# Gated mix of a spectral filter and an MLP on one core: dense products of the first chunk ahead of the first DFT tiles, and VectorE's exchange of halves partly on ScalarE

## The chip, the core and the metric

The kernel runs on one core of a Trainium2 chip. The metric is the device time of one execution in microseconds (us); lower is better. The core has five engines that each work through their own instructions in order: TensorE (PE, with PEld its weight loads), VectorE (DVE), ScalarE (ACT), GpSimd (POOL) and SyncE (SP). Here SP issues nearly all DMA transfers, which 16 DMA engines carry out; POOL does nothing.

## What is computed

```python
def reference(A_x, A_w_r, A_w_i, B_x, B_w1, B_b1, B_w2, B_b2, gate_w):
    x = A_x                                     # [1, 2048, 512]
    g = sigmoid((x * gate_w).sum(-1, keepdims=True))
    X = rfft2(x, axes=(-2, -1)) * (A_w_r + 1j * A_w_i)
    a = irfft2(X, s=(2048, 512), axes=(-2, -1))
    h = gelu(einsum("bsd,df->bsf", x, B_w1) + B_b1)      # F = 1792
    b = einsum("bsf,fd->bsd", h, B_w2) + B_b2
    return g * a + (1 - g) * b
```

Both branches read the same 2048 tokens of 512 features: the spectral branch filters over tokens and features by DFTs, the dense branch is a two-layer MLP, and a gate per token mixes them.

## The kernel before

**Precision.** Every operand of a matrix product is split into a high and a low part (`split`, L407 to 412: ScalarE copies to the high part, VectorE subtracts to get the low part), and a product is three matmuls: high by high, high by low, low by high (`prods`, L371). All matmuls are recorded at one line, L369, so the profile tells them apart by the names of their tiles.

**Spectral branch.** The 2048 tokens are 16 tiles of 128 (`forward(j)`, L495), done in the order `NORD` = 0, 4, 8, 12, 1, 5, 9, 13, 2, ... For each tile VectorE forms sums and differences of mirrored features (`eo`, L502), ScalarE and VectorE split them (`eoh` L507, `eol` L509), TensorE does the DFT over features (`pd`, 12 matmuls of 258 columns, with the table `cf`), ScalarE and VectorE split the result (`xh` L539, `xl` L540), and TensorE does a DFT of 128 over tokens (`py`, 6 matmuls with a table `tf` loaded for each tile). ScalarE copies one half of it (`pys`, L559); VectorE adds (L560) and subtracts (L563) into the tile `Y[j]`. The subtraction exchanges the lower and upper 64 partitions, so it is two instructions of 64 partitions. The first two rows of every tile pair go by a small DMA to `own` (L565); `own_rows` (L571) corrects them by a small product (`pown`) and 16 small DMAs put them back (L589). Radix-4 butterflies over the 16 tiles, the filter (`filt`, L671), and butterflies back (`stage4`, L706) are all VectorE's; then come the inverse products `pz` and `pa` (`inverse`, L710), where `v` and `z` are the split operands.

**Dense branch.** The MLP (`mlp`, L782) works in 4 chunks of 512 tokens and two halves of the hidden features (7 blocks of 128 each). For each half and chunk: 7 `ph` (12 matmuls of 512 columns; gelu at L803, then a split into `g`), then 4 `po` of 7 x 3 matmuls. The split tokens of a chunk (`mxh`, `mxl`) are made from four tiles (`split_1`, L475; for chunk 0 from the tiles 0, 4, 8, 12 that the spectral branch loads too), stored to memory (`keep_x`, L481) and read again for the second half of the hidden features (L493). Weights are loaded and split on the way (`load_w`, L777; `wa`, `wb`; two landing buffers of each kind). Partial sums go through memory (`bacc`).

**What sets the order.** No loop order is executed as written. Every operation is a `Step` with an engine, an assumed cost, a lag, buffers and a rank (`Graph.add`, L150), and a planner (`schedule`, L188) simulates the engines: an engine that is free takes the ready step of lowest rank whose buffers find a slot. The result is one fixed order of instructions for each engine. `slots` (L320) says how many buffers of each kind there are, `most` (L324) how many of them a class may hold. Ranks are `FEED` = 1, `BULK` = 5, `EARLY` = 0.5, `FIRST` = 0.3 for the first three tiles. Semaphores that make an instruction wait are put in behind the planner. The DMA transfers go round a set of eight semaphores, so a ninth transfer is issued only when an earlier one has landed.

At the start eight matmuls of zeros (`warm`, L424) run on TensorE while the tables `cf` (L434), four weights and the first tile (by ScalarE's queue, L432) are loaded; then the first tile's `pd` follows.

Of the kernel before, what the change touches and what calls it, by code (L numbers as in the profile page):

```python
# [17 lines left out]
P = 128  # L18
# [112 lines left out]

class Step:
# [11 lines left out]
class Graph:  # L144
# [5 lines left out]
    def add(self, eng, cost, lag, emit, reads=(), writes=(), rank=1):  # L150
# [4 lines left out]
        def parts(x):  # L155
            b, p = x if isinstance(x, tuple) else (x, None)
            return b, range(len(b.wrote)) if p is None else (p,)
# [149 lines left out]
def tile_kernel(ctx: ExitStack, tc: tile.TileContext, xt, w1, w2, b1, b2, x0g, wf, wrev, out, consts):  # L307
# [12 lines left out]
    slots = {"xr": 3, "wra": 2, "wrb": 2, "t2k": 6, "e2": 4, "z": 4, "ttab": 3, "xhl": 2, "wa": 2 * FA, "wb": 2 * FA, "hid": 2 * FA,  # L320
# [3 lines left out]
    most = {("pm", "ph"): 2, ("pm", "po"): 2, ("pm", "py"): 3}  # L324
# [12 lines left out]

    FIRST, FEW = 0.3, 3
# [20 lines left out]
    def dma(emit, kb, reads, writes, rank=FEED):  # L359
        return add("sp", kb / 390, 2.2, emit, reads, writes, rank)  # L360

    def dma_act(emit, kb, reads, writes):
        return add("act", 0.4, kb / 390 + 2.2, emit, reads, writes, 0)
# [40 lines left out]
    def t2k(name, n=ND, cls=None):  # L404
        return buf("t2k", [P, 2, n], F32, name, cls=cls)
# [26 lines left out]
    dma_act(lambda: act.dma_start(x0.ap().rearrange("p a b -> p (a b)")[:, :NQ * P + NQ], x0g), 258, [], [x0])  # L432
    for c in range(2):
        dma(lambda c=c: raw(cf(c, 0), cf_d[c]), 272, [], [(cft, k) for k in (c, 8 + c, 10 + c)], 0)  # L434
    XF[NORD[1]] = load_x(NORD[1], "f")

    def tiny(emit, reads, writes):
        return add("vec", 0.1, 0.1, emit, reads, writes, -1)
# [42 lines left out]
    def keep_x(c):  # L481
        for k, b in zip("hl", X[0, c]):
            dma(lambda k=k, b=b: sp.dma_start(xs[c, k].ap(), b.ap().bitcast(F32)), 1024, [b], [xs[c, k]], 6)
# [11 lines left out]
    def forward(j):  # L495
        first = j == 0
        feed = FIRST if j in NORD[:FEW] else FEED
# [3 lines left out]
        for s, op in ((0, ALU.add), (1, ALU.subtract)):  # L501
            v(lambda s=s, op=op: vec.tensor_tensor(eo.ap()[:, s], x.ap()[:, 0:2], x.ap()[:, 2:4], op=op), 256, [x],  # L502
              [(eo, s)], -1 if first else feed)
        for k in (0, 1) if first else (slice(0, 2),):
# [3 lines left out]
              -1 if first else feed)  # L508
            v(lambda k=k: vec.tensor_tensor(l.ap()[:, k], eo.ap()[:, k], h.ap()[:, k], op=ALU.subtract),  # L509
              256 * len(ps), sub[0] + sub[1], sub[2], feed)  # L510
# [35 lines left out]
        pys = t2k(f"pys{j}", cls="pys")  # L546
# [12 lines left out]
        a(lambda: act.activation(pys.ap()[:, 0], py[0].ap()[:, :ND], AF.Copy), 257, [py[0]], [pys], 0)  # L559
        v(lambda: vec.tensor_tensor(Y[j].ap()[:, 0], py[1].ap()[:, :ND], pys.ap()[:, 0], op=ALU.add), 257, [py[1], pys], [(Y[j], 0)], 0)  # L560
        lo, up = slice(0, HP), slice(HP, P)
        for k, (o, i) in enumerate(((lo, up), (up, lo))):
            v(lambda o=o, i=i: vec.tensor_tensor(Y[j].ap()[o, 1], py[1].ap()[i, :ND], pys.ap()[i, 0], op=ALU.subtract),  # L563
              257, [pys, py[1]], [(Y[j], 1 + k)], 0)
# [3 lines left out]
    own = buf("bb", [2 * NJ, 2, NE], F32, "own", parts=NJ + 1)  # L568
    add("vec", 0.1, 0.1, lambda: vec.memset(own.ap()[:, :, ND:], 0.0), [], [(own, NJ)], 3)

    def own_rows():  # L571
        t = buf("ttab", [2 * NJ, 2, 2, 2, 2 * NJ], F32R, "fx")
        dma(lambda: raw(t.ap(), fx_d), 32, [], [t], 3)
        oh, ol = (buf("z", [2 * NJ, 2, 512], F32R, f"own{k}") for k in "hl")
        a(lambda: act.activation(oh.ap()[:, :, :NE], own.ap(), AF.Copy), 514, [own], [oh], 2)
        v(lambda: vec.tensor_tensor(ol.ap()[:, :, :NE], own.ap(), oh.ap()[:, :, :NE], op=ALU.subtract), 514, [own, oh], [ol], 2)
# [8 lines left out]
        m(fix, NE, 12, [t, oh, ol], [ps], FEED)  # L585
        r = t2k("ownr")
        a(lambda: act.activation(r.ap()[:2 * NJ], ps.ap()[:, :, :ND], AF.Copy), 514, [ps], [r], 2)
# [189 lines left out]
    def load_w(n, f):  # L777
        t = buf("wr" + n, [P, D], F32, f"w{n}r{f}")
        dma(lambda: sp.dma_start(t.ap(), (w1 if n == "a" else w2)[f]), 256, [], [t], EARLY if f < FA else 2)
        W[n, f] = split(f"w{n}{f}", "w" + n, [P, D], t, lambda x: x, 512, EARLY if f < FA else 3)  # L780

    def mlp(half, c):  # L782
# [23 lines left out]
        for q in range(NQ):  # L806
# [3 lines left out]
            for n in (slice(0, 2 * P), slice(2 * P, 4 * P)) if end else (slice(0, 4 * P),):  # L810
                ps = buf("pm", [P, n.stop - n.start], F32, f"po{half}_{c}{q}{n.start}", pool=pp, cls="po")
# [35 lines left out]

    ORDER = (2, 3, 0, 1)
    LATE = (0, 1)

    for n, j in enumerate(NORD):
# [3 lines left out]
        if j == 12:  # L855
            keep_x(0)
# [6 lines left out]
    for p0 in range(0, P, 32):  # L863
# [3 lines left out]
            700, [gsc], [gt])  # L867
# [75 lines left out]
```

## Time and profile before

| | |
|---|---|
| median of 3 runs | 402.66 us (401.99 to 402.69) |
| the profiled execution | 402.02 us, of which its span 400.2 us |
| TensorE busy | 388.6 us, 97% of the span |
| VectorE busy | 328.4 us, 82% |
| ScalarE busy | 162.4 us, 41% |
| DMA | 65.63 MB, mean 164 GB/s |
| granted TensorE clock | 0.994 |

The page's numbers come from one execution. Its span runs from the first to the last instruction; the time of the execution is 1.8 us longer. Busy shares are averages over stages. The chain of work that ended last is followed back from the last instruction; a row of it gives start, duration and the work. Rows in order of time give start, duration, engine, line, operation, output and inputs, and in brackets the idle time before them with what ended it. SPq and ACTq are the queues on which DMA transfers are issued. In the first slices the clock column reads 1.00 although matmuls take twice their later time, so the durations are the better guide there.

### The profile page before, as it was taken

The page shows a single profiled execution, that of the slowest core. Times are in us where ns is not written, and L with a number is a line of the kernel's source. Part 1 is how long each engine was busy: PE and PEld are TensorE (multiplying, and loading weights), DVE is VectorE, ACT ScalarE, POOL GpSimd, SP SyncE. Part 2 cuts the span into 40 slices and gives each one's busy share as a digit, 9 for nine tenths or more (in the row PEclk, how much of TensorE's full clock was granted, in tenths as well). Part 3 has the DMA queues.
Part 4 walks back from the last instruction along what each step waited for, and adds up shares of the span by engine and source line. Part 5 has one row for each costly group of instructions (what it writes and reads, how often), then busy time and mean ns, then how long its engine had stood idle before and what let it go on. Part 6 is the DMA issues. An engine that isn't in the chain of part 4 may idle for free.

```text
span 400.2 us, 5515 instructions
## 1 busy us (share of the span) xinstructions
PE 388.6 (97%) x1961; PEld 329.5 (82%) x1961; DVE 328.4 (82%) x687; ACT 162.4 (41%) x267; POOL 0.2 (0%) x4
## 2 busy tenths in 40 slices
PE   7789999999999999999999999999999999999996
PEld 5668889887888888888888898888899888888885
DVE  4998999999999999999999779987999996322223
ACT  5567555636651354156236520334422354004300
POOL 0000000000000000000000000000000000000000
PEclk9998999999999999999999999999999999999999
DMA  8896455696049133743952285451756444510011
GB/s 294 330 316 199 138 156 159 176 382 212 5 109 359 64 104 131 266 141 95 312 178 102 79 311 164 134 162 47 261 153 176 154 126 150 231 52 26 2 52 52
DMA packets 31675, 65.63 MB, mean 164 GB/s; under 512 B 3744, under 2 KB 10240, under 8 KB 29600
## 3 DMA queue, kind: packets, MB, share of 16 engines
q1 hardware_dynamic: 31504, 65.03, 48.9%
q8 instruction: 15, 0.25, 0.2%
q10 hardware_dynamic: 144, 0.26, 0.2%
q14 instruction: 12, 0.10, 0.1%
HBM read 46.26 MB, written 18.88 MB: 163 GB/s over the span
## 4 chain that ended last, share of the span: by engine, by line
PE 79%; DVE 12%; DMA 5%; issue 2%; ACT 1%; SPq 0%; DVEq 0%; ACTq 0%
PE ph L369 34%; PE po L369 33%; PE pz L369 6%; PE pa L369 3%; PE pd L369 2%; DVE y L563 2%; DVE eo L502 2%; DVE eol L509 1%; DMA war<-in_w 1%; DVE y L560 1%; DMA cf<-cf 1%; DMA xs0h<-mxh 1%; DMA bb<-bacc 1%; DMA ba<-bacc 1%; PE py L369 1%
## 5 line engine op out<-in xcount | busy, mean ns | idle before, releaser
L803 ACT ACTIVATE ph<-ph,b1t 128x512 f32<-128x512 f32 x56 | 37.0, 661 | 85.1 <-PE ph L369 83.7
L823 ACT ACTIVATE o<-po,b2t 128x512 f32<-128x512 f32 x16 | 11.0, 690 | 46.2 <-PE po L369 43.2
L836 DVE SCALAR_TENSOR_TENSOR o<-gb,po 128x512 f32<-128x512 f32 (+1 forms) x9 | 5.7, 629 | 24.5 <-PE po L369 24.5
L688 DVE TENSOR_TENSOR m<-y,wf 128x514 f32<-128x514 f32 x32 | 21.4, 690 | 0.0
L369 PE MATMUL pd<-cf,eoh 128*128 128x258 f32 x128 | 19.3, 295 | 2.0 <-ACT eoh L507 1.9
L369 PEld LDWEIGHTS pd<-cf,eoh 128*128 128x128 f32 x128 | 17.2, 198 | 3.7 <-ACT eoh L507 3.6
L563 DVE TENSOR_TENSOR y<-py,pys 64x257 f32<-64x257 f32 x32 | 13.6, 424 | 0.4
L369 PE MATMUL pd<-cf,eol 128*128 128x258 f32 x64 | 11.4, 303 | 2.3 <-DVE eol L509 2.2
L759 DVE SCALAR_TENSOR_TENSOR ba<-gb,ba 128x512 f32<-128x512 f32 x16 | 11.0, 688 | 2.3 <-DMA ba<-bacc 2.3
L369 PEld LDWEIGHTS pd<-cf,eol 128*128 128x128 f32 x64 | 9.2, 200 | 3.3 <-DVE eol L509 3.3
L502 DVE TENSOR_TENSOR eo<-xf 128x256 f32<-128x256 f32 x32 | 11.8, 419 | 0.1
L507 ACT ACTIVATE eoh<-eo 128x512 fp32r<-128x512 f32 (+1 forms) x17 | 10.1, 600 | 4.1 <-DVE eo L502 4.1
L729 DVE TENSOR_TENSOR zg<-pz,gb 128x512 f32<-128x512 f32 x16 | 11.0, 688 | 0.7 <-PE pz L369 0.4
L509 DVE TENSOR_TENSOR eol<-eo,eoh 128x512 fp32r<-128x512 f32 (+1 forms) x17 | 11.0, 653 | 0.0
L559 ACT ACTIVATE pys<-py 128x257 f32<-128x257 f32 x16 | 6.2, 385 | 9.7 <-PE py L369 9.4
L744 ACT ACTIVATE od<-pa 128x512 f32<-128x512 f32 x8 | 4.8, 596 | 11.1 <-PE pz L369 4.4
L478 DVE TENSOR_TENSOR mxl<-xm,mxh 128x512 fp32r<-128x512 f32 x12 | 7.8, 685 | 0.4 <-ACT mxh L477 0.4
L411 DVE TENSOR_TENSOR g_13l<-ph,g_13h 128x512 fp32r<-128x512 f32 x4 | 2.8, 690 | 6.1 <-ACT g_13h L410 6.1
L560 DVE TENSOR_TENSOR y<-py,pys 128x257 f32<-128x257 f32 x16 | 6.8, 422 | 0.9 <-ACT pys L559 0.9
L477 ACT ACTIVATE mxh<-xm 128x512 fp32r<-128x512 f32 x12 | 7.1, 626 | 0.7 <-DMA xm<-in_xt 0.5
L369 PE MATMUL ph<-mxh,wa3h 128*128 128x512 f32 x16 | 7.0, 435 | 0.0
L369 PE MATMUL ph<-mxl,wa3h 128*128 128x512 f32 x16 | 6.8, 424 | 0.0
(654 smaller groups left out, 1286.5 us busy)
## 6 DMA issues: line engine op xcount, KB each, us to landing
bacc<-o SPq DMA_DIRECT2D x24, 256.0 KB
ti<-ti SPq DMA_DIRECT2D x16, 384.0 KB
wf<-in_wf SPq DMA_DIRECT2D x16, 257.0 KB
tf<-tf SPq DMA_DIRECT2D x16, 256.0 KB
ba<-bacc SPq DMA_DIRECT2D x16, 256.0 KB
xf<-in_xt SPq DMA_DIRECT2D x15, 256.0 KB
war<-in_w SPq DMA_DIRECT2D x14, 256.0 KB
wbr<-in_w SPq DMA_DIRECT2D x14, 256.0 KB
```

The costliest lines, as they stand in the source:

```text
L369: pe.matmul(ps, w, x, start=start, stop=stop)
L478: v(lambda: vec.tensor_tensor(l.ap()[:, :, j1], x.ap()[:, :NQ], h.ap()[:, :, j1], op=ALU.subtract), 512, [x, (h, j1)], [(l, j1)], rank)
L502: v(lambda s=s, op=op: vec.tensor_tensor(eo.ap()[:, s], x.ap()[:, 0:2], x.ap()[:, 2:4], op=op), 256, [x], [(eo, s)], -1 if first else feed)
L507: a(lambda k=k: act.activation(h.ap()[:, k], eo.ap()[:, k], AF.Copy), 256 * len(ps), sub[0], sub[1], -1 if first else feed)
L509: v(lambda k=k: vec.tensor_tensor(l.ap()[:, k], eo.ap()[:, k], h.ap()[:, k], op=ALU.subtract), 256 * len(ps), sub[0] + sub[1], sub[2], feed)
L560: v(lambda: vec.tensor_tensor(Y[j].ap()[:, 0], py[1].ap()[:, :ND], pys.ap()[:, 0], op=ALU.add), 257, [py[1], pys], [(Y[j], 0)], 0)
L563: v(lambda o=o, i=i: vec.tensor_tensor(Y[j].ap()[o, 1], py[1].ap()[i, :ND], pys.ap()[i, 0], op=ALU.subtract), 257, [pys, py[1]], [(Y[j], 1 ...
L688: v(lambda mk=mk, k=k, y=y, w=w: vec.tensor_tensor(mk.ap(), y.ap(), w.ap()[:, k:k + 1].to_broadcast([P, 2, ND]), op=ALU.mult), 514, [y, w] ...
L729: vec.tensor_tensor(zg.ap()[:, :, :, n], ps.ap().rearrange("p a (b c) -> p a b c", b=2), bcast(gj, 2, 2), op=ALU.mult)
L759: vec.scalar_tensor_tensor(ba[k].ap(), gg, 1.0, ba[k].ap(), op0=ALU.subtract, op1=ALU.mult)
L803: a(lambda f=f, ps=ps: act.activation(ps.ap(), ps.ap(), AF.Gelu_apprx_tanh, bias=b1t.ap()[:, f:f + 1]), 600, [b1t], [ps]).table = "gelu"
L823: a(lambda o=o, ps=ps, q=q: act.activation(o.ap(), ps.ap(), AF.Identity, bias=b2t.ap()[:, q:q + 1]), 600, [b2t, ps], [o])
```

## The change

- **First chunk ahead.** Tiles 4, 8 and 12 are loaded first on SP (tile 0 on ScalarE's queue as before), then the first four weights, and only then the `cf` tables; ranks are set so that the split of the four tiles and the first two `ph` come ahead of the first tile's DFT. In the planned order TensorE does the zeros, `ph_0`, `ph_1`, the first tile's `pd` and `py`, `ph_2`, and goes on in a mix of both.
- **Zeros.** 18 matmuls of zeros instead of 8.
- **Split tokens.** `keep_x` stores each of the two halves in four pieces of 256 KB (512 runs of 512 bytes each) instead of one of 1024 KB; for chunk 0 it also waits until tile 9 has gone through the forward DFT.
- **Exchange of halves.** For the 12 tiles after the first four (`BY_ACT`) VectorE does one subtraction on 128 partitions (L578 of the changed kernel) and ScalarE copies the two halves crosswise (L581).
- **Own rows.** The 16 tiles `Y[j]` lie in one buffer `yy`. Four DMAs store the edge rows of four tiles each to `ywas` in memory, one gathers them to `own`, one stores the corrected rows to `yfix`, and four bring them back. The table `fx` is laid out for that order.
- **Planner.** `t2k` has 8 buffers instead of 6, the first `po` has a class of its own with one buffer, the assumed DMA rate is 340 instead of 390 and its lag 2.8 instead of 2.2; the gate's broadcast loads get rank 4.

```diff
--- before.py
+++ after.py
-    fx = np.zeros((NJ, 2, 2, NJ, 2, 2))
+    fx = np.zeros((2, NJ, 2, 2, NJ, 2))
...
-                    fx[n, r, c, n % 4 + 4 * q] = np.stack([o.real, o.imag], 1)
+                    fx[r, n, c, :, n % 4 + 4 * q] = np.stack([o.real, o.imag], 1)
...
+class View:
+    def __init__(self, buf, lo, n, view):
+        self.buf, self.lo, self.n, self.view = buf, lo, n, view
+
+    def ap(self):
+        return self.view(self.buf.ap())
...
-    slots = {"xr": 3, "wra": 2, "wrb": 2, "t2k": 6, "e2": 4, "z": 4, "ttab": 3, "xhl": 2, "wa": 2 * FA, "wb": 2 * FA, "hid": 2 * FA,
+    slots = {"xr": 3, "wra": 2, "wrb": 2, "t2k": 8, "e2": 4, "z": 4, "ttab": 3, "xhl": 2, "wa": 2 * FA, "wb": 2 * FA, "hid": 2 * FA,
...
-    most = {("pm", "ph"): 2, ("pm", "po"): 2, ("pm", "py"): 3}
+    most = {("pm", "ph"): 2, ("pm", "po"): 2, ("pm", "po0"): 1, ("pm", "py"): 3}
...
-    FIRST, FEW = 0.3, 3
...
     def dma(emit, kb, reads, writes, rank=FEED):
-        return add("sp", kb / 390, 2.2, emit, reads, writes, rank)
+        return add("sp", kb / 340, 2.8, emit, reads, writes, rank)
...
-    Y = [one(f"y{j}", [P, 2, ND], parts=3) for j in range(NJ)]
+    yy = one("y", [P, NJ, 2, ND], parts=3 * NJ)
+    Y = [View(yy, 3 * j, 3, lambda t, j=j: t[:, j]) for j in range(NJ)]
...
-    xs = {(c, k): one(f"xs{c}{k}", [P, NQ, 4, P], pool=dp) for c in range(4) for k in "hl"}
+    xs = {(c, k): one(f"xs{c}{k}", [P, NQ, 4, P], pool=dp, parts=4) for c in range(4) for k in "hl"}
...
-        dma(lambda: sp.dma_start(x.ap(), xt[j]), 256, [], [x])
+        dma(lambda: sp.dma_start(x.ap(), xt[j]), 256, [], [x], j / 100 if tag == "f" and j in NORD[:4] else FEED)
...
-        for _ in range(8):
+        for _ in range(18):
             mm(none.ap(), zero.ap(), bcast(zero.ap(), 4), True, True)
 
-    add("pe", 3.5, 0.1, warm, [zero], [none], 0)
+    add("pe", 6.2, 0.1, warm, [zero], [none], 0)
...
+    for j in NORD[1:4]:
+        XF[j] = load_x(j, "f")
     for c in range(2):
-        dma(lambda c=c: raw(cf(c, 0), cf_d[c]), 272, [], [(cft, k) for k in (c, 8 + c, 10 + c)], 0)
-    XF[NORD[1]] = load_x(NORD[1], "f")
+        dma(lambda c=c: raw(cf(c, 0), cf_d[c]), 272, [], [(cft, k) for k in (c, 8 + c, 10 + c)], 0.6)
...
     def keep_x(c):
+        late = [Y[NORD[6]]] if c == 0 else []
         for k, b in zip("hl", X[0, c]):
-            dma(lambda k=k, b=b: sp.dma_start(xs[c, k].ap(), b.ap().bitcast(F32)), 1024, [b], [xs[c, k]], 6)
+            for j in range(4):
+                dma(lambda k=k, b=b, j=j: sp.dma_start(xs[c, k].ap()[:, :, j], b.ap()[:, :, j].bitcast(F32)), 256,
+                    [(b, j), *late], [(xs[c, k], j)], 6)
...
     def forward(j):
-        feed = FIRST if j in NORD[:FEW] else FEED
...
-              [(eo, s)], -1 if first else feed)
+              [(eo, s)], FEED)
...
-        pys = t2k(f"pys{j}", cls="pys")
+        pys = t2k(f"pys{j}", cls="pys", parts=2)
...
-        lo, up = slice(0, HP), slice(HP, P)
-        for k, (o, i) in enumerate(((lo, up), (up, lo))):
-            v(lambda o=o, i=i: vec.tensor_tensor(Y[j].ap()[o, 1], py[1].ap()[i, :ND], pys.ap()[i, 0], op=ALU.subtract),
-              257, [pys, py[1]], [(Y[j], 1 + k)], 0)
-        dma(lambda: sp.dma_start(own.ap()[2 * j:2 * j + 2, :, :ND], Y[j].ap()[0:P:HP]), 4, [Y[j]], [(own, j)], 3)
+        halves = ((0, HP), (HP, 0))
+        if j in BY_ACT:
+            v(lambda: vec.tensor_tensor(pys.ap()[:, 1], py[1].ap()[:, :ND], pys.ap()[:, 0], op=ALU.subtract), 257, [py[1], (pys, 0)],
+              [(pys, 1)], 0)
+            for k, (o, i) in enumerate(halves):
+                a(lambda o=o, i=i: act.activation(Y[j].ap()[o:o + HP, 1], pys.ap()[i:i + HP, 1], AF.Copy), 257, [(pys, 1)], [(Y[j], 1 + k)], 0)
+        else:
+            for k, (o, i) in enumerate(halves):
+                add("vec", 0.45, 0.1, lambda o=o, i=i: vec.tensor_tensor(
+                    Y[j].ap()[o:o + HP, 1], py[1].ap()[i:i + HP, :ND], pys.ap()[i:i + HP, 0], op=ALU.subtract),
+                    [(pys, 0), py[1]], [(Y[j], 1 + k)], 0)
+        if j // 4 == 3:
+            dma(lambda: sp.dma_start(ywas.ap()[:, j % 4::4], yy.ap()[0:P:HP, j % 4::4]), 16, [Y[k] for k in range(j % 4, NJ, 4)],
+                [(ywas, j % 4)], 0)
+
+    ywas, yfix = (one(f"y{k}", [2, NJ, 2, ND], pool=dp, parts=4) for k in ("was", "fix"))
...
     def own_rows():
...
+        dma(lambda: sp.dma_start(own.ap()[:, :, :ND], ywas.ap().rearrange("r j c n -> (r j) c n")), 64, [ywas], [(own, 0)], 0)
...
-        for j in range(NJ):
-            dma(lambda j=j: sp.dma_start(Y[j].ap()[0:P:HP], r.ap()[2 * j:2 * j + 2]), 4, [r], [Y[j]], 3)
+        dma(lambda: sp.dma_start(yfix.ap().rearrange("r j c n -> (r j) c n"), r.ap()[:2 * NJ]), 64, [r], [yfix], 0)
+        for k in range(0, NJ, 4):
+            dma(lambda k=k: sp.dma_start(yy.ap()[0:P:HP, k:k + 4], yfix.ap()[:, k:k + 4]), 16, [yfix], Y[k:k + 4], 0)
...
     def load_w(n, f):
-        dma(lambda: sp.dma_start(t.ap(), (w1 if n == "a" else w2)[f]), 256, [], [t], EARLY if f < FA else 2)
+        dma(lambda: sp.dma_start(t.ap(), (w1 if n == "a" else w2)[f]), 256, [], [t], (0.2 if f == 0 and n == "a" else EARLY) if f < FA else 2)
...
+    BY_ACT = NORD[4:]
...
-        if j == 12:
-            keep_x(0)
+    keep_x(0)
...
-            700, [gsc], [gt])
+            700, [gsc], [gt], 4)
```

More of the change, by code (lines that the diff above doesn't have):

```diff
@@ L156, in parts @@
             b, p = x if isinstance(x, tuple) else (x, None)
+            if isinstance(b, View):
+                return b.buf, range(b.lo, b.lo + b.n) if p is None else (b.lo + p,)
             return b, range(len(b.wrote)) if p is None else (p,)
@@ L359, in dma @@
     def dma(emit, kb, reads, writes, rank=FEED):
-        return add("sp", kb / 390, 2.2, emit, reads, writes, rank)
+        return add("sp", kb / 340, 2.8, emit, reads, writes, rank)
     def dma_act(emit, kb, reads, writes):
-        return add("act", 0.4, kb / 390 + 2.2, emit, reads, writes, 0)
+        return add("act", 0.4, kb / 340 + 2.8, emit, reads, writes, 0)
     def raw(dst, src, q=sp):
@@ L432, in tile_kernel @@
     dma_act(lambda: act.dma_start(x0.ap().rearrange("p a b -> p (a b)")[:, :NQ * P + NQ], x0g), 258, [], [x0])
+    for j in NORD[1:4]:
+        XF[j] = load_x(j, "f")
     for c in range(2):
-        dma(lambda c=c: raw(cf(c, 0), cf_d[c]), 272, [], [(cft, k) for k in (c, 8 + c, 10 + c)], 0)
-    XF[NORD[1]] = load_x(NORD[1], "f")
+        dma(lambda c=c: raw(cf(c, 0), cf_d[c]), 272, [], [(cft, k) for k in (c, 8 + c, 10 + c)], 0.6)
     def tiny(emit, reads, writes):
-        return add("vec", 0.1, 0.1, emit, reads, writes, -1)
+        return add("vec", 0.1, 0.1, emit, reads, writes, 0.7)
     for k, op in enumerate((ALU.add, ALU.subtract)):
@@ L507, in forward @@
             a(lambda k=k: act.activation(h.ap()[:, k], eo.ap()[:, k], AF.Copy), 256 * len(ps), sub[0], sub[1],
-              -1 if first else feed)
+              FEED)
             v(lambda k=k: vec.tensor_tensor(l.ap()[:, k], eo.ap()[:, k], h.ap()[:, k], op=ALU.subtract),
-              256 * len(ps), sub[0] + sub[1], sub[2], feed)
+              256 * len(ps), sub[0] + sub[1], sub[2], FEED)
         if j % 4 == 0:
@@ L583, in fix @@
                           c == 0, c == 1)
-        m(fix, NE, 12, [t, oh, ol], [ps], FEED)
-        r = t2k("ownr")
-        a(lambda: act.activation(r.ap()[:2 * NJ], ps.ap()[:, :, :ND], AF.Copy), 514, [ps], [r], 2)
-        for j in range(NJ):
-            dma(lambda j=j: sp.dma_start(Y[j].ap()[0:P:HP], r.ap()[2 * j:2 * j + 2]), 4, [r], [Y[j]], 3)
+        m(fix, NE, 12, [t, oh, ol], [ps], 0)
+        r = t2k("ownr", cls="own")
+        a(lambda: act.activation(r.ap()[:2 * NJ], ps.ap()[:, :, :ND], AF.Copy), 514, [ps], [r], 0)
+        dma(lambda: sp.dma_start(yfix.ap().rearrange("r j c n -> (r j) c n"), r.ap()[:2 * NJ]), 64, [r], [yfix], 0)
+        for k in range(0, NJ, 4):
+            dma(lambda k=k: sp.dma_start(yy.ap()[0:P:HP, k:k + 4], yfix.ap()[:, k:k + 4]), 16, [yfix], Y[k:k + 4], 0)
     def fma(o, x, s, b, n, reads, writes):
@@ L810, in mlp @@
             for n in (slice(0, 2 * P), slice(2 * P, 4 * P)) if end else (slice(0, 4 * P),):
-                ps = buf("pm", [P, n.stop - n.start], F32, f"po{half}_{c}{q}{n.start}", pool=pp, cls="po")
+                ps = buf("pm", [P, n.stop - n.start], F32, f"po{half}_{c}{q}{n.start}", pool=pp, cls="po0" if half == c == q == 0 else "po")
                 for f in fs:
```

16 lines of the change are left out of this document (8 added, 8 removed).

## Prediction

> **What bounds the kernel now.** I read the page first, then the chain of work that ended last, then busy time by ten-microsecond stretches, then the start in order of time. The page:
>
> ```profile
> span 400.2 us, 5515 instructions
> ...
> PE 388.6 (97%) x1961; PEld 329.5 (82%) x1961; DVE 328.4 (82%) x687; ACT 162.4 (41%) x267; POOL 0.2 (0%) x4
> ...
> PE   7789999999999999999999999999999999999996
> ...
> DVE  4998999999999999999999779987999996322223
> ```
>
> TensorE is nearly always busy; only its first three slices fall off, and there VectorE is at nine tenths. So the end is TensorE's work plus what it loses. The chain gives both (start, duration, work):
>
> ```profile
> 5.89 2.96 PE pd L369 x12
> ...
> 9.07 0.61 ACT x0h L539
> 9.71 0.70 DVE x0l L540
> ...
> 30.50 4.16 PE ph L369 x12
> 34.66 0.72 PE py L369 x6
> 35.38 1.44 PE pd L369 x12
> ...
> 80.13 11.59 PE po L369 x51
> 91.72 1.54 PE pown L369 x12
> ...
> 94.15 19.05 PE ph L369 x84
> 113.20 19.04 PE po L369 x84
> ...
> 219.28 1.43 PE pz L369 x12
> ...
> 230.36 1.43 PE pa L369 x12
> ...
> 254.32 0.70 DVE v3l L411
> 255.07 2.90 PE pz L369 x22
> ...
> 377.16 19.32 PE po L369 x105
> ```
>
> Useful work at full rate: 16 blocks of 84 dense products at 19.04 (0.227 each) are 304.6; 16 `pd` at 1.44, 23.0; 16 `py` at 0.72, 11.5; 16 `pz` and 8 `pa` at 1.43, 34.3; `pown` 1.54. Sum **375.1 us**. Everything else is loss. By 80.13 the order has finished all DFT products, a block of `ph` and 30 `po`: 19.04 + 6.8 + 23.0 + 11.5 = 60.4, so **19.7 us** are lost there. From 80.13 to TensorE's end (377.16 + 19.32 = 396.48) 316.35 us pass for 314.7 of work: 1.7 lost. A tail of 3.7 follows. 375.1 + 19.7 + 1.7 + 3.7 = 400.2.
>
> Inside the 19.7: up to 35.38 only four tiles' `pd` and `py` and four `ph` are done, 8.6 + 10.9 = 19.5, so 15.9 are lost (a start at 5.89, first products at half rate, 2.96 for 1.44; waits; a `ph` at 4.16 for 2.72). Between 35.38 and 80.13 it is 44.75 - 40.9 = 3.9, and there VectorE is the full queue:
>
> ```profile
> 40.00:50.00 10.00, 10.00 (x62) 8.86 (x62) 9.57 (x24) 5.03 (x10) 0.00 (x0) 1.00 0.45 137
> 50.00:60.00 10.00, 9.67 (x66) 8.68 (x66) 9.76 (x25) 5.46 (x12) 0.00 (x0) 1.00 0.52 156
> 60.00:70.00 10.00, 9.91 (x71) 9.10 (x71) 9.30 (x23) 5.82 (x12) 0.00 (x0) 1.00 0.51 159
> 70.00:80.00 10.00, 9.49 (x59) 8.04 (x58) 9.67 (x23) 6.46 (x12) 0.00 (x0) 1.00 0.60 175
> ```
>
> The columns after the length are PE, PEld, DVE, ACT, POOL, clock, DMA share, GB/s.
>
> **The change, part by part.** *The start.* TensorE's order becomes 18 zero products, `ph_0`, `ph_1`, the first tile, `ph_2`, the second tile's high half, and so on. `ph_0` needs four token tiles and one weight, each loaded and split. The start in order of time:
>
> ```profile
> 0.73 0.81 SPq L366 DMA_DIRECT2D cf<-cf  x2
> ...
> 1.05 3.78 PE L369 MATMUL none<-zero 128*128 128x512 f32 x8 [1.05 <-DVE zero L422]
> ...
> 4.27 0.42 ACT L455 ACTIVATE cf<-cf 128x256 fp32r<-128x256 f32 x1 [1.85 <-DMA cf<-cf]
> 4.47 0.80 SPq L366 DMA_DIRECT2D tf<-tf  x2
> ...
> 5.12 0.42 ACT L455 ACTIVATE cf<-cf 128x256 fp32r<-128x256 f32 x1 [0.43 <-DMA cf<-cf]
> ...
> 6.05 0.61 ACT L477 ACTIVATE mxh<-xf 128x512 fp32r<-128x512 f32 x1
> 6.57 0.61 ACT L410 ACTIVATE wa0h<-war 128x512 fp32r<-128x512 f32 x1
> ...
> 13.73 0.33 SPq L483 DMA_DIRECT2D xs0h<-mxh  x1
> ...
> 17.67 0.33 SPq L483 DMA_DIRECT2D xs0l<-mxl  x1
> ...
> 20.17 0.68 DVE L411 TENSOR_TENSOR wa1l<-war,wa1h 128x512 fp32r<-128x512 f32 x1
> ...
> 20.77 0.68 DVE L411 TENSOR_TENSOR wb1l<-wbr,wb1h 128x512 fp32r<-128x512 f32 x1
> ```
>
> and a stretch of it, with what the DMA engines moved:
>
> ```profile
> 6.00:8.00 2.00, 2.00 (x10) 2.00 (x11) 1.39 (x4) 1.71 (x4) 0.00 (x0) 1.00 1.06 398
> ```
>
> Today the first queued load and the first token tile, sent together, are there at 4.27; the next load follows 0.85 us later, and at 398 GB/s 256 KB take 0.66. In the new order the first two tiles are there at 4.2, the third by 4.9 to 5.1, the fourth by 5.5 to 5.9, the weight by 6.2 to 6.8. On SyncE's queue the `cf` tables go behind four weights, and the ninth load in all waits until an earlier one has landed (today `tf`, at 4.47); at the same rates they are there at about 10. ScalarE then needs 0.5 (queued pitch, 6.05 to 6.57) to 0.6 and VectorE 0.60 (20.17 to 20.77) to 0.7 each, six and five operations in turn: the weight's low half is ready at about 8.1. Only the third product reads it, so `ph_0` counts as started at 8.1 - 2 x 0.227 = **7.7**, 1.8 later than today's first product.
>
> The zeros must not outlast that. Eight took 3.78, so 18 end at 9.6 if the clock never rises and at 1.05 + 3.78 + 10 x 0.227 = 7.1 if it rises after the eighth. Today the twelve `pd` from 5.89 still ran at half rate after a break of one microsecond. I take 7.7 and keep 9.2 (full rate only from 8.85, where today's slow products end) for the range. The Trainium skill ("TensorE: Matmul & The Clock Gate", part 1) says that a free-running window of about 3.4 us must be full of activity before the full clock is granted; as an estimate that ends the zeros between 6.6 and 8.3. The trace agrees in that eight zeros and a break did not suffice.
>
> Then `ph_0` and `ph_1` take 5.44 and `pd` 1.44, to 14.6 (the tables and their four small edits are done by about 12). The first tile's `py` must wait for `x0h` (0.61) and `x0l` (0.70), and VectorE has one weight split (0.60) queued ahead of `x0l`: the six `py` end at about 16.5 instead of 15.3. So at 16.5 there is 7.6 of work done, **8.9 lost**. From there to the fourth tile dense blocks lie between tiles; I add 0.5.
>
> *The rest of the DFT stage.*
>
> ```profile
> L563 DVE TENSOR_TENSOR y<-py,pys 64x257 f32<-64x257 f32 x32 | 13.6, 424 | 0.4
> L560 DVE TENSOR_TENSOR y<-py,pys 128x257 f32<-128x257 f32 x16 | 6.8, 422 | 0.9 <-ACT pys L559 0.9
> L559 ACT ACTIVATE pys<-py 128x257 f32<-128x257 f32 x16 | 6.2, 385 | 9.7 <-PE py L369 9.4
> ```
>
> In 12 tiles two half-height subtracts (0.85) become one of full height (0.42): VectorE has 12 x 0.43 = 5.1 us less, in the stretch where it is the full queue. ScalarE gets 24 copies of about 0.385, 9.2 us; its rows above show 22.8 busy of 40. The copies feed no DFT product, but `x h` and `eo h` queue behind them. Bounds for this stretch: 3.9 lost as today, 0 if VectorE's relief is passed on whole, 3.9 + 4.6 if ScalarE's queue holds back half of the tiles by a pair of copies (12 x 0.385). I take 3.2, near the row of today. Loss to the last DFT product: 8.9 + 0.5 + 3.2 = **12.6** instead of 19.7.
>
> *Stores of split tokens in pieces.* 32 pieces of 256 KB replace eight stores of 1024 KB, each piece 512 runs of 512 bytes. The first eight leave the busy start (today two go at 13.7 and 17.7) for the time of tiles 2 to 15, where the DMA share is 0.45 to 0.60. A piece costs between 0.66 (the rate above) and several times that; no row has runs so short. I cost them at nothing: half the DMA time is free, and the slots that they release are next written by the `xm` splits, which I place 4 us or more behind them.
>
> *Own rows.* 16 small stores and 16 small loads become four stores, a gather, one store and four loads; `pown` now stands behind `ph_3` of the second chunk, some 11 us of work later. Its chain is two transfers longer (some 3 us each by the 3.5 us of the first queued load, 0.73 to 4.27), so it is covered. If not, TensorE waits the difference: 0 to 1. Each of the four stores holds SyncE until ScalarE's copies of its tile are done, with tables and token loads queued behind; they are due two to three tiles (some 8 us) later, so a hold of 2 us costs nothing.
>
> *Behind the front.* Today v3 sets the chain (254.32 to 255.07). It is due after 234.3 us of TensorE work, in the new order after 245.9; with 7.1 less lost that is 4.5 us later on the clock, and VectorE has 5.1 less to do. I leave the 1.7 and the tail of 3.7. The extra two `t2k` slots and the own class for the first `po` cost nothing: they are the planner's.
>
> **Sum.** 375.1 + 12.6 + 1.7 + 3.7 = 393.1 span. The profiled execution took 402.02, 1.8 more than its span: 394.9. The median of the runs shown is 402.66 (401.99 to 402.69), 0 to 0.7 above that execution; I say **395.2**.
>
> **Rivals.** (1) *ScalarE becomes the queue that is late*: 4.6 more, **399.8**. For it: 9.2 us of copies in an in-order queue that feeds every tile twice. Against: with them it is at 32 of 40. Chance 0.14.
> (2) *The clock falls again.* In today's trace `ph` at 30.50 took 4.16, and the products just before it had waited longest:
>
> ```profile
> PE pd L369 <- DVE eol L509: 2.2, 3, 1.5
> ```
>
> Of the 2.2 us in three waits, one was 1.5; the new first tile holds waits of 0.7 and 0.4 close together. Price 4.16 - 2.72 = 1.4: **396.6**. The page named above has the clock fall only after a whole idle window of about 3.4 us, which would leave the new start at full rate; the `ph` row speaks against it. Chance 0.12, inside the range.
> (3) *The gain is given back at v3*: VectorE's chain there does not move up, TensorE waits for it, about **402**, no change. Against: v3 is due later. Chance 0.06.
> (4) *Slower: the short runs clog the DMA queues.* Ten pieces go while tiles 6 to 15 load 12 x 256 KB (7.9 us) in some 18 us. Up to 1.0 us a piece they fit; every microsecond above delays the tables by ten. At 1.8 us a piece the gain of 7.1 is gone; at 2.6, **411**. The nearest rows, 2 KB runs at 398 GB/s, give 0.66. Chance 0.10. The Trainium skill ("DMA: Bandwidth & Descriptors", Specifications) puts the least run for line rate at 512 bytes; by that rule a piece keeps 0.66 and this rival falls. No row of this trace has such runs.
>
> **How the numbers follow.** The forecast has 0.58. Its own ends: full relief of VectorE and no late loss give 392; zeros to 9.2 and 3.9 lost give 397.5. With (1) the range is 392.0 to 400.0; (3) and (4) lie outside, and a little of either tail. A measurement of this kernel can tell about 0.2% from no change, 0.8 us. Faster: 0.58 + 0.12 + 0.14 = 0.84; same 0.06; slower 0.10.
>
> **What would show it.** In the new profile `ph_0` should start near 7.3 and run without a break from 8.1; the last `py` (61.8 of work in) should end near 74.4 (today 80.1); VectorE's group of half-height subtracts should be x8. Four stretches of dense work after 100 should still take 19.04. I am wrong if `ph_0` starts after 9, if PE shows waits for `x h` above 4 us in sum, if the DMA share from 45 to 70 is near 1, or if v3's `pz` waits several microseconds.

## The result, and the profile after

The changed kernel takes **397.69 us** (median of 4 runs, 397.49 to 397.81); the kernel before, beside it, 402.33 (401.89 to 402.69). The ratio is 0.9885, interval 0.9868 to 0.9902: 1.15% faster, 4.6 us. The forecast was 395.2 with a range of 392.0 to 400.0. The profiled execution took 397.49 with a span of 395.7, again 1.8 apart. In several of the kernels below the executions fall in two groups, 1.5 to 2 us apart, with a mean granted clock of 0.995 or 0.996 in most of the longer and 0.998 to 1.000 in the shorter; "at full clock" means the shorter.

The page of the changed kernel:

```profile
span 395.7 us, 5566 instructions
...
PE 387.7 (98%) x1971; PEld 329.3 (83%) x1971; DVE 322.1 (81%) x675; ACT 172.3 (44%) x291; POOL 0.2 (0%) x4
...
PE   8899999999999999999999999999999999999996
...
DVE  5889888899499999999999957986599999952223
...
DMA packets 47444, 65.77 MB, mean 166 GB/s; under 512 B 4113, under 2 KB 26993, under 8 KB 46385
```

TensorE's first slices rose from 7 to 8; VectorE has 6.3 us less, ScalarE 9.9 more. The chain of work that ended last, with the same points as before:

```profile
7.41 0.70 DVE wa0l L422
...
8.15 5.30 PE ph L379 x22
13.46 1.45 PE pd L379 x12
...
14.92 0.61 ACT x0h L554
...
15.56 0.16 DVE logit L557
15.72 0.60 DVE wa2l L422
16.32 0.62 DVE x0l L555
...
16.98 0.40 PE py L379
...
21.07 4.16 DMA wbr<-in_w
25.25 0.63 ACT wb5h L421
25.89 0.50 ACT x4h L554
...
26.48 0.68 DVE wb5l L422
27.16 0.60 DVE x4l L555
...
33.57 5.74 PE ph L379 x24
...
63.83 5.52 DMA tf<-tf
...
69.48 0.62 PE py L379 x3
...
77.66 10.91 PE po L379 x48
```

Read it as before: time less useful work in TensorE's order is what is lost. At 17.38 (end of the first tile's `py`) 7.6 of work is done: 9.8 lost. At 33.57, 21.56: 12.0. At 77.66, behind the last `py`, 61.76: **15.9** (19.7 before). Between 33.57 and 77.66, 3.9 is lost, to the tenth what the prediction found for that stretch before. So all that the front gained was gained by the end of the fourth tile. TensorE's largest waits over the whole span (us in total, times, longest), beside that for the zeros:

```profile
PE py L379 <- DMA tf<-tf: 0.7, 1, 0.7
PE py L379 <- ACT x0h L554: 0.7, 1, 0.7
PE py L379 <- DVE x0l L555: 0.6, 1, 0.6
PE py L379 <- ACT pys L574: 0.5, 1, 0.5
```

A wait for a table is new. Three windows of the changed kernel, columns as before:

```profile
20.00:30.00 10.00, 9.83 (x63) 8.64 (x62) 8.85 (x17) 7.42 (x15) 0.00 (x0) 1.00 0.66 192
...
45.00:58.00 13.00, 12.90 (x84) 11.40 (x83) 11.05 (x32) 9.74 (x22) 0.00 (x0) 1.00 0.57 168
58.00:70.00 12.00, 11.29 (x81) 10.13 (x80) 10.30 (x26) 9.49 (x21) 0.00 (x0) 1.00 1.07 353
```

Between 58 and 70 us the DMA engines are full, and TensorE loses 0.7 of 12 us. In that stretch a `tf` table lands 5.5 us after its issue (median of 4), over the whole run 3.6.

Behind the front nothing moved against the forecast. Rows of the chain from there:

```profile
99.44 1.54 PE pown L379 x12
...
128.40 19.04 PE ph L379 x84
...
262.25 2.87 PE pz L379 x24
...
372.75 19.32 PE po L379 x105
```

From 77.66 to 392.07 314.4 us pass for 313.3 of work (375.1 - 61.8): 1.1 lost where 1.7 was said, and a tail of 3.6.

### The profile page after: what moved, and what is told of

Same layout as the page of the kernel before. It is cut to its first block, busy times and chain, and to the rows that moved or that the text cites. A ratio compares the mean times of both kernels' runs of the same rounds, so it can differ in the third digit from the quotient of the medians.

```text
span 395.7 us, 5566 instructions
## 1 busy us (share of the span) xinstructions
PE 387.7 (98%) x1971; PEld 329.3 (83%) x1971; DVE 322.1 (81%) x675; ACT 172.3 (44%) x291; POOL 0.2 (0%) x4
## 4 chain that ended last, share of the span: by engine, by line
PE 90%; DVE 4%; DMA 3%; ACT 1%; issue 1%
PE po L379 38%; PE ph L379 37%; PE pz L379 6%; PE pd L379 4%; PE pa L379 3%; PE py L379 2%; DMA tf<-tf 1%; DMA wbr<-in_w 1%; DMA xf<-in_xt 1%; DVE y L584 1%; DVE mxl L490 0%; PE pown L379 0%; DVE y L575 0%; ACT pys L574 0%; DVE wa0l L422 0%
## 5 line engine op out<-in xcount | busy, mean ns | idle before, releaser
L379 PE MATMUL pd<-cf,eoh 128*128 128x258 f32 x128 | 17.9, 283 | 0.0
L781 DVE TENSOR_TENSOR u<-pa,od 128x512 f32<-128x512 f32 x8 | 5.5, 688 | 7.4 <-ACT od L771 7.4
L581 ACT ACTIVATE y<-pys 64x257 f32<-64x257 f32 x24 | 10.0, 418 | 3.5 <-DVE pys L578 3.2
L786 DVE SCALAR_TENSOR_TENSOR ba<-gb,ba 128x512 f32<-128x512 f32 x16 | 10.9, 683 | 0.0
L771 ACT ACTIVATE od<-pa 128x512 f32<-128x512 f32 x8 | 4.8, 598 | 13.7 <-PE pa L379 13.1
L379 PE MATMUL pd<-cf,eol 128*128 128x258 f32 x64 | 10.4, 284 | 0.0
L557 DVE TENSOR_REDUCE logit<-pd 128x1 f32<-128x2 f32 x16 | 2.5, 155 | 6.1 <-ACT x0h L554 1.3
L379 PE MATMUL none<-zero 128*128 128x512 f32 x18 | 6.4, 527 | 1.0 <-DVE zero L433 1.0
```

Source lines behind the costliest of these rows:

```text
L379: pe.matmul(ps, w, x, start=start, stop=stop)
L581: a(lambda o=o, i=i: act.activation(Y[j].ap()[o:o + HP, 1], pys.ap()[i:i + HP, 1], AF.Copy), 257, [(pys, 1)], [(Y[j], 1 + k)], 0)
L786: vec.scalar_tensor_tensor(ba[k].ap(), gg, 1.0, ba[k].ap(), op0=ALU.subtract, op1=ALU.mult)
```

## The experiments

Theory 1: the gain is the start's, and what was missed in it is the first tiles' chain of small steps. Theory 2: the stores that were put off take part of it back. The rival to both is the exchange of halves, as gain (VectorE) or as cost (ScalarE). Each kernel is the changed one with the edit shown. The kernel before, run beside each, had medians of 401.63 to 401.98. Losses are read from each trace as above.

**1. Eight zeros.**

```diff
-        for _ in range(18):
+        for _ in range(8):
```

> The changed kernel with 8 products of zeros instead of 18; the planner still counts them as 6.2 us, so every queue keeps the order of the changed kernel. If the 18 zeros keep the clock up: TensorE stands still from 4.8 to 7.3, ph_0 then runs at half rate (0.43 instead of 0.23 each) for 7 to 12 products, 1.5 to 2.7 us lost: 399.2 to 400.4. Rival: the third product waits for the weight's low half until 8.1 anyway and the clock does not fall: 397.5 to 398.0.

Measured: 399.16 us (398.29 to 400.25), ratio 0.9933 (0.9909 to 0.9957); 1.5 more. TensorE starts `ph_0` earlier, but from 8.6 to 11.6 us its products stand 0.43 apart, twice their pitch. The start of it:

```profile
6.92 0.50 PE L379 MATMUL ph<-mxh,wa0h 128*128 128x512 f32 x1 [2.09 <-ACT wa0h L421]
7.36 0.51 PE L379 MATMUL ph<-mxl,wa0h 128*128 128x512 f32 x1
```

The ten zeros are worth 1.5 us by the medians. In the profiled execution (398.29, the shortest of the five) the last `py` ends at 78.46, 0.8 later than in the changed kernel.

**2. Runs of 2 KB.** The chunk copies are laid out so that a piece is 128 runs of 2 KB; the order of every engine stays.

```diff
-    xs = {(c, k): one(f"xs{c}{k}", [P, NQ, 4, P], pool=dp, parts=4) for c in range(4) for k in "hl"}
+    xs = {(c, k): one(f"xs{c}{k}", [P, 4, NQ, P], pool=dp, parts=4) for c in range(4) for k in "hl"}
...
-                dma(lambda k=k, b=b, j=j: sp.dma_start(xs[c, k].ap()[:, :, j], b.ap()[:, :, j].bitcast(F32)), 256,
+                dma(lambda k=k, b=b, j=j: sp.dma_start(xs[c, k].ap()[:, j], b.ap()[:, j].bitcast(F32)), 256,
```

> The changed kernel with the split tokens laid out tile by tile, in SBUF and in memory, so that a piece of 256 KB is 128 runs of 2 KB instead of 512 runs of 512 bytes; order and costs of the planner are unchanged, the dense products read their moving operand in four stretches of 128. If the short runs clog the DMA queues: the DMA share between 58 and 70 us falls from 1.1 to about 0.7, the 0.7 us wait of py for its table at 69.5 goes, 396.6 to 397.1. Rival, that the bytes and not the runs fill the queues: share, wait and 397.7 stay.

Measured: 397.37 us (396.58 to 398.93), ratio 0.9892 (0.9867 to 0.9917), no difference from the changed kernel's 0.9885. The window of 58 to 70 us:

```profile
58.00:70.00 12.00, 11.95 (x84) 10.79 (x83) 11.02 (x29) 10.03 (x23) 0.00 (x0) 1.00 0.92 338
```

The engines' share is 0.92 at 338 GB/s for 1.07 at 353: the short runs take some 11% more of the engines' time for a byte, but that hardly reaches TensorE. A `tf` table lands no sooner with long runs (6.1 us between 45 and 70, 5.5 before), and its wait shrinks only from 0.7 to 0.4. Run 1, with short runs, has no such wait at all. So neither theory nor rival came out whole. The Trainium skill ("DMA: Bandwidth & Descriptors", Specifications) holds 512 bytes enough for line rate; the rates of 353 and 338 GB/s agree with that, the 11% does not quite.

**3. No exchange on ScalarE.**

```diff
-    BY_ACT = NORD[4:]
+    BY_ACT = []
```

> The changed kernel without the exchange of halves on ScalarE (all 16 tiles do two subtractions of 64 partitions on VectorE). If VectorE's relief of 5.1 us is what counts: 401 to 403, with the losses between the ph_4 block and the last py rising from 3.9 to 7 to 9 us. If the gain is the start's: 397.5 to 398.5, with the same losses.

Measured: 397.42 us (396.81 to 398.02), ratio 0.9886 (0.9862 to 0.991): no difference in the medians, with ScalarE at 5.3 of 12 us between 58 and 70 for 9.5. The losses between `ph_4` and the last `py` neither rose nor stayed: they fell to 2.9, for 3.9, and there is no wait for `tf`. This profile also shows the second rival of the prediction. After the first tile's waits TensorE's products stand 0.43 apart, twice their pitch:

```profile
15.78 0.75 PE L379 MATMUL py<-x0h,tf 128*128 128x258 f32 x4 [0.69 <-ACT x0h L554]
17.18 0.51 PE L379 MATMUL py<-x0l,tf 128*128 128x258 f32 x2 [0.65 <-DVE x0l L555]
17.77 0.65 PE L379 MATMUL ph<-mxh,wa2h 128*128 128x512 f32 x1
18.22 0.63 PE L379 MATMUL ph<-mxl,wa2h 128*128 128x512 f32 x1
18.64 0.63 PE L379 MATMUL ph<-mxh,wa2l 128*128 128x512 f32 x1
```

The changed kernel's own profile has the same two waits, and there the products that follow stand 0.23 apart.

**4. The old start.** The start of before (order of loads, ranks, 8 zeros, `cf` first) in the changed kernel.

```diff
-    for _ in range(18):
+    for _ in range(8):
...
-    for j in NORD[1:4]:
-        XF[j] = load_x(j, "f")
...
-              [(eo, s)], FEED)
+              [(eo, s)], -1 if first else feed)
```

> The changed kernel with the start of before (tables first, first tile's DFT ahead of the dense part, 8 zeros, ranks of before); exchange, pieces, late stores and own rows as changed. If the gain is the start's (12.0 us lost by the ph_4 block instead of 15.9): 401.2 to 402.2. If it is VectorE's relief: 397.7 to 399.

Measured: 400.82 us (400.26 to 402.42), ratio 0.9985 (0.9969 to 1.0001). That is just under the range given for the start. Without its start the change is worth some 0.6 us, not told apart from nothing; the start is worth 3.1. The profiled execution (402.1, one of three near 402) has lost 17.5 by `ph_4`. Theory 1 holds in its first half.

**5. The first tile's gap filled.** Five steps are moved in the planned order, each to the place just ahead of the second step named, so that `pd` of tile 4 lies between `x0h` and `x0l`.

```diff
+    move(("eoh", 4), ("xh", 0))
+    move("wa2l", ("logit", 0))
+    move(("eol", 4), ("logit", 0))
+    move(("high", 4), ("py", 0, 0))
+    move(("low", 4), ("py", 0, 0))
```

> The changed kernel, with five steps put elsewhere in the emitted order and nothing else: ScalarE copies tile 4's fold ahead of x0h, VectorE subtracts wa2l and then tile 4's fold ahead of the first logit, and TensorE does pd of tile 4 (1.44 us) ahead of py of tile 0. Theory (what is lost up to the first tile's py is the chain pd, x0h, x0l, g_0l, with nothing to do beside it: the two waits of 0.69 and 0.65 us and 0.19 us after them): pd of tile 4 fills them, no wait over 0.3 us is left before ph_2, ph_2 starts near 17.3 with 1.4 us more work done, and the last py ends near 76.3: 396.2 us. Rival (the front is set by VectorE and ScalarE, so a gap that is filled opens again before x4h, x8h or the weights): the waits of TensorE up to 35 us stay the same in sum, last py again near 77.7, 397.5 us.

Measured: 398.9 us (396.75 to 399.43), ratio 0.9921 (0.989 to 0.9952). Four of the six executions have a clock of 0.995 or 0.996; the profiled one (397.39) is of the two at full clock. There the two waits are gone, one as long as both stands at the next tile, and the last `py` ends at 77.53:

```profile
15.37 1.21 PE L379 MATMUL pd<-cf,eoh 128*128 128x258 f32 x8 [0.30 <-ACT eoh L523]
...
26.38 0.75 PE L379 MATMUL py<-x4h,tf 128*128 128x258 f32 x4 [1.49 <-ACT x4h L555]
```

The rival held. `x4h` stands behind copies of weights in ScalarE's queue, and these wait for loads:

```profile
23.36 0.63 ACT L422 ACTIVATE wb4h<-wbr 128x512 fp32r<-128x512 f32 x1 [0.94 <-DMA wbr<-in_w]
24.50 0.63 ACT L422 ACTIVATE wa5h<-war 128x512 fp32r<-128x512 f32 x1 [0.51 <-DMA war<-in_w]
```

**6. Stores not put off.** The first chunk's pieces are bound to their own data only.

```diff
-        late = [Y[NORD[6]]] if c == 0 else []
+        late = []
```

> The changed kernel with keep_x's pieces of the first chunk bound to nothing but their own data (no Y of the seventh tile among what they read), so that 2 MB of stores go out from some 13 us on, between the weight loads, and not from 52.9 to 62.4. Theory A (in 58 to 70 us, where the DMA share is 1.07 at 353 GB/s, it is these bytes together with the next chunk's that make tf late): the tf waits of 0.7 us near 69 go, DMA share 58 to 70 falls to some 0.6, and the time falls by 0.7 to 1: 396.8 us. Theory B (the early weights need the queues): the loads of wa3 to wb7 land later by what the stores take, 2 MB at some 300 GB/s are 7 us of which most falls on idle shares (0.66 in 20 to 40 us), TensorE waits 1 to 3 us more between 18 and 40: 398.5 to 400.5 us.

Measured: **394.93 us** (394.53 to 396.32), ratio 0.9837 (0.9812 to 0.9863), 2.8 us under the changed kernel. Of theory A the wait for `tf` is gone and the share came down as said, but the gain is three times as large, and not all of it can be theory A's (below). The pieces go out from 11.0 to 19.1 us instead of 52.9 to 62.4; the engines are full at 20 to 30 and no longer at 58 to 70:

```profile
20.00:30.00 10.00, 9.83 (x56) 8.55 (x55) 7.84 (x18) 5.36 (x12) 0.00 (x0) 0.91 0.95 323
...
58.00:70.00 12.00, 11.83 (x89) 11.13 (x88) 11.20 (x30) 10.52 (x24) 0.00 (x0) 1.00 0.65 211
```

No weight came too late, which theory B had expected. The waits up to 90 us, beside those for the zeros and of the first tile:

```profile
PE py L379 <- DVE x10l L555: 0.2, 1, 0.2
PE py L379 <- DVE x4l L555: 0.2, 1, 0.2
```

The clock of 0.91 shows that the clock fell in this execution; from `ph_2`'s start to the next `pd` 4.4 us pass, for 2.9 in the changed kernel. So the profile (396.25) is 1.5 above the four executions from 394.53 to 394.94, and even so its last `py` ends at 76.42, 1.2 ahead of the changed kernel's.

By place: up to `ph_4` 12.4 is lost, 10.9 without the 1.5 of the clock, for 12.0 in the changed kernel; from there to the last `py` 2.2 for 3.9. So some 1.1 of the gain lies ahead of 34 us, where none of the late stores has yet gone (the first goes at 52.9). It can't be their relief. The planner's order there is another: ScalarE copies `x4h` ahead of the weights, where the changed kernel's chain has it behind `wb5h`, and the wait of 0.5 for `pys` is gone.

```profile
27.16 0.60 ACT L554 ACTIVATE x4h<-pd 128x516 fp32r<-128x516 f32 x1 [2.52 <-PE pd L379]
27.66 0.62 ACT L421 ACTIVATE wa4h<-war 128x512 fp32r<-128x512 f32 x1
28.18 0.62 ACT L421 ACTIVATE wb4h<-wbr 128x512 fp32r<-128x512 f32 x1
```

No run has this order with late stores (run 9 moves `x4h` alone), so that the order makes these 1.1 us is argued, not shown.

**7. Three edits at once:** runs 2, 3 and 5 together.

> Three edits in the changed kernel together: the five steps moved as in the run before the last, the chunk pieces laid out in runs of 2 KB, and every exchange of halves back on VectorE (BY_ACT empty). If the last two cost and gain nothing, as their single runs had it, and the first gains 1.3 us: 396.2 us, as the moved steps alone. If the queue's relief (0.92 for 1.07 in 58 to 70) and ScalarE's (5.3 of 12 us for 9.5) count once the front is shorter: 395.2 us. If the filled gap gains nothing, 397.4 us.

Measured: 397.18 us (396.57 to 397.54), ratio 0.9882 (0.9859 to 0.9905). With the stores put off, none of the three gains, and `x4h` is waited for 1.5 us again.

**8. Early stores and the filled gap:** runs 5 and 6 together.

> The changed kernel with the stores of the first chunk not put off (as in the run of early stores, 394.93 us) and the five steps moved that put pd of tile 4 between x0h and x0l (as in the run of the filled gap). Theory (with the stores early the planner puts x4h ahead of wa4h to wb5h in ScalarE's order, so the wait of 1.5 us for x4h that took back the filled gap has no load in front of it): no wait of TensorE over 0.3 us up to 35 us, the clock not under 1.00 in any slice after 8 us, last py some 1.4 us earlier than with early stores at full clock (near 73.5): 393.4 us. Rival (the front is limited by work of VectorE and ScalarE, not by the order): the wait opens again before x4h or x8h, 394.9 us.

Measured: **394.66 us** (393.95 to 396.47), ratio 0.9825 (0.98 to 0.9849), the least of all and under both kernels; not told apart from run 6. Theory and rival each have half. The waits (profiled execution: 394.66):

```profile
PE py L379 <- DVE x4l L556: 1.0, 1, 1.0
PE pd L379 <- ACT eoh L523: 1.0, 1, 1.0
```

The clock stays at 1.00 and the last `py` ends at 74.84, but two waits of 1.0 took the place of 0.7 and 0.6, one ahead of tile 4's `pd` and one ahead of its `py`.

**9. The gap filled and `x4h` ahead of `wb4h`,** stores late: one move more than in run 5.

```diff
+    move(("xh", 4), "wb4h")
```

> The changed kernel with its late stores, the five steps moved as in the run of the filled gap, and one more: ScalarE copies x4h ahead of wb4h, so that it doesn't stand behind the copies that wait for weight loads (0.94, 0.51 us in that run, 1.40 in the changed kernel). Theory (x4h behind a load took the gain back): the wait of 1.5 us goes, and the run is 1.2 to 1.5 us under the filled gap's fast mode (397.4, 396.75), near 395.7 us. Rival (late stores set the loss from 35 us on, and what is gained before is lost again by the waits for tf and pys): 397 us.

Measured: 398.14 us (397.2 to 399.98), ratio 0.9916 (0.9889 to 0.9942): no gain. TensorE's waits:

```profile
PE py L379 <- DMA tf<-tf: 1.5, 1, 1.5
PE py L379 <- DVE x4l L556: 1.4, 1, 1.4
PE pd L379 <- ACT eoh L523: 1.1, 2, 0.8
```

`x4h` was not waited for any more; `x4l`, behind `wb5l` in VectorE's queue, was, and the wait for `tf` was twice the changed kernel's.

**10 and 11. Early stores without the exchange,** with the gap filled and without: `BY_ACT = []` in run 8 and in run 6.

> As the first of this call, and all exchanges of halves on VectorE (BY_ACT empty). If VectorE's 5.1 us in the DFT tiles are hidden even in the shorter front: the same as the first within 0.6 us (393.4). If ScalarE's exchange pays once the stores no longer crowd 58 to 70 us (VectorE 11.2 of 12 us there in the run of early stores): 1 to 3 us slower, 394.5 to 396.

> The changed kernel with the stores of the first chunk not put off, and all exchanges of halves on VectorE (BY_ACT empty); the first tile as in the changed kernel. With late stores the exchange was worth nothing (397.42 without, 397.69 with); with early stores and the filled gap the run without it was 1.8 us slower (396.48 for 394.66). Theory (the exchange pays only where VectorE and not the late stores set the pace of the DFT tiles): 396.5 us, 1.5 over the run of early stores. Rival (that 1.8 us came from another start or order of that one kernel): 395 us.

Measured: 396.48 us (396.18 to 397.75), ratio 0.9874 (0.9852 to 0.9895), 1.8 over run 8; and 397.73 us (396.05 to 397.95), ratio 0.9896 (0.9866 to 0.9926), 2.8 over run 6, of which half is the clock (two executions at 1.000: 396.05 and 396.16; four at 0.996: 397.67 to 397.95). At full clock the four cases stand so (the shorter executions of runs 3, 6, 11, 12 and of the changed kernel's first measurement):

| | exchange on ScalarE | on VectorE |
|---|---|---|
| stores late | 396.9 to 398.2 | 396.8 to 397.0 |
| stores early | 394.5 to 394.9 | 396.1 to 396.2 |

By the medians of these executions the exchange is worth about 1.3 us with early stores (394.8 for 396.1) and costs about 0.9 with late ones (397.7 for 396.9); late stores cost 2.9 us with it and 0.8 without. The cells hold two to nine executions, from up to three chips, those on VectorE two each. The traces divide it by place (us lost, run by run; runs 5, 7, 8 and 10 have the gap filled):

| | up to `ph_4` | from there to the last `py` |
|---|---|---|
| late, on ScalarE (changed kernel, runs 12 and 5) | 12.0, 12.3, 12.1 | 3.9, 3.9, 3.7 |
| late, on VectorE (runs 3 and 7) | 12.0, 12.4 | 2.9, 2.9 |
| early, on ScalarE (runs 6 and 8) | 10.9, 10.8 | 2.2, 2.3 |
| early, on VectorE (runs 11 and 10) | 10.9, 11.0 | 3.7, 3.6 |

From runs 3 and 6 the 1.5 of the fallen clock is taken off. The front of every kernel with early stores gains 1.1 to 1.4 on its fellow with late ones. Behind it, where the late stores go, the kernels with late stores lose 1.4 to 1.7 more with the exchange, but 0.7 to 0.8 less without it. On VectorE more dense work lies ahead of the last `py`; counted up to 84 us in all, these differences stay the same to 0.2.

**12. The changed kernel again,** on the chip of run 11.

> The changed kernel itself, word for word, so that the runs with early stores have it on the same chip beside them: 397.7 us; over 397 if putting the stores off costs what the earlier runs say (2.7 us), near 395.5 if much of that was the difference between two chips.

Measured: 397.92 us (396.93 to 399.09), ratio 0.9907 (0.9879 to 0.9934). The changed kernel is no faster on this chip, and on the chip of run 6 the late stores of runs 2 and 3 stood at 397.4. So the gain of run 6 is not a difference between chips.

## Why the prediction was right, and where it was not

The sign, the place and the range were right; the time was 2.5 us too low. By its own steps:

- **The start of `ph_0`: right.** Said: near 7.3, counted 7.7, third product waiting for the weight's low half at 8.1. Found: 7.27, that half at 7.41 to 8.11, third product at 8.15, counted 7.70. The zeros ended at 7.44 (1.05 + 6.39; said 7.1 if the clock rises after the eighth, 9.6 if never). Run 1 shows that the ten more of them keep the rate up, run 4 that the start carries the gain.
- **The end of the first tile: 8.9 said, 9.8 found.** `pd` ended 0.3 later (14.91 for 14.6), and a logit reduction as well as the weight's subtract stands between `x0h` and `x0l`. The mechanism was right, its size was off.
- **"From there to the fourth tile ... I add 0.5": this step failed, and by the most: 2.2 was lost.** It took dense blocks between the tiles for cover. In the chain above `wb5h` waits for a load of 4.16 us, `x4h` and `x4l` stand behind it and `wb5l` in queues that work in order, and from there VectorE works without a gap up to `ph_4`. Of the 2.2, TensorE's largest single wait is the 0.5 for `pys` ahead of the fourth tile's `py`, and 0.2 is for `x4l`; the rest is spread over smaller gaps. Runs 5 and 9 did not remove the loss by moving steps at one place: a filled gap of 1.3 us opened again before `x4h`, and then before `x4l`. The runs with early stores, whose order there is another, lose 1.1 to 1.4 less by `ph_4`.
- **"The rest of the DFT stage", 3.2: 3.9 found.** The relief of VectorE was there (eight half-height subtracts of 3.4 us and twelve of full height, 5.0, for 13.6), and the rows of ScalarE came out as said, a copy 418 ns for 385:

```profile
L581 ACT ACTIVATE y<-pys 64x257 f32<-64x257 f32 x24 | 10.0, 418 | 3.5 <-DVE pys L578 3.2
...
L584 DVE TENSOR_TENSOR y<-py,pys 64x257 f32<-64x257 f32 x8 | 3.4, 424 | 0.1
```

  But the relief did not reach the end: with late stores the stretch loses 1.0 less without the exchange (run 3). Runs 6, 8, 10 and 11 show that it is worth 1.3 to 1.8 us with early stores. That 3.2 lies so near 3.9 is in part luck, for the two effects nearly cancel.
- **"Stores of split tokens in pieces ... I cost them at nothing": this step failed too, but less than the time of run 6 says.** Sending them early gains 2.8 us, the size of the whole miss, yet 1.1 of it lies ahead of 34 us, where the late stores have not begun. In the stretch in which they go the changed kernel loses 1.7 more than run 6, of which the wait for `tf` is 0.7; without the exchange late stores lose 0.8 less there (runs 3 and 11). The prediction counted that the pieces fit in the free half of the DMA time, and that was so; it priced bytes and not the delay of what queues between them (`tf` 5.52 us in the chain). The sign that it had named, a DMA share near 1 between 45 and 70, came for 12 of these 25 us. Its fourth rival had the place right and the mechanism wrong: the length of the runs (run 2) did not matter much.
- **Own rows, v3, the dense blocks: right.** TensorE waits for neither `own` nor v3; blocks of 84 still take 19.04. The late loss was 1.1 for 1.7.

The sum: 375.1 + 15.9 + 1.1 + 3.6 = 395.7, the span. Against the 393.1 said, 0.9 + 1.7 + 0.7 more was lost up to the last `py`, and 0.6 + 0.1 less behind it.

The second rival, the clock that falls at the first tile, did not happen in the changed kernel's profile, and does in others (runs 3 and 6) at the price that was named, 1.4 (found 1.5). Rival 3 did not happen: v3 came in time. Nor did rival 1 at its price of 4.6: removing the copies changes the median by 0.3 us (run 3), at full clock by some 0.9, a cost of its sign and a fifth of its size.

What stays open: which step of the other order gains in the front, and why, behind `ph_4`, kernels with late stores lose more with the exchange and less without it. Run 6 changes the hour of 2 MB and, through the planner, the order of some steps on every engine. Run 2 lowers the DMA share in the same order and loses 0.4 less behind `ph_4`; run 3 has a share of 0.99 at 303 GB/s between 58 and 70 with TensorE busy for 11.97 of 12, and run 1 a share of 1.05 with 11.95. So a full queue alone is not the cause; that it is what happens to be due in it is argued, not shown. By place, run 8 against the changed kernel: lost up to `ph_2`'s start 9.0 for 10.0 (the filled gap), to `ph_4`'s 10.8 for 12.0, to `ph_6`'s 11.4 for 13.0, to the last `py` 13.1 for 15.9. Why the same two waits let the clock fall in one execution and not in the next isn't settled either.

## What to carry to other kernels

A store without a reader nearby is not free where you put it off to: look for loads that someone needs at once in that stretch, and try it ahead of them too. When such an edit goes through a planner, read the gain by place before you name its cause: a gain that lies ahead of the stretch which the stores left is not the relief of that stretch. A gap in a chain through queues that work in order may open again at the next tile if that tile's steps stand behind the same late load; move one step and look where the wait comes back. And an edit that measures nothing may be masked by another: the exchange was worth nothing until the stores had moved.

## What the runs showed of the hardware that was not expected

- The clock can fall to half rate behind two waits of 0.69 and 0.65 us that lie 1.4 us apart (run 3: products 0.43 apart from 17.77 on; granted clock 0.90 and 0.93 in the windows of 10 to 20 and 20 to 30). In the changed kernel the same waits left it at 1.00. The Trainium skill ("TensorE: Matmul & The Clock Gate", part 1) has it fall after an idle window of about 3.4 us; run 3 had no such window, its longest wait there being 0.69, so the measurement differs from the page.
- With the stores in runs of 512 bytes the DMA engines moved 353 GB/s for 12 us at a share of 1.07; with runs of 2 KB (run 2) 338 GB/s at 0.92, some 10% less of their time for a byte.
